# Newton steps ahead of the gate product, landmark products and second query scores at other half steps, a later split

## The chip, the cores and the metric

The kernel runs on one core of a Trainium2 chip. TensorE (PE) does the matrix products into PSUM, VectorE (DVE) and ScalarE (ACT) read and write PSUM and SBUF, GpSimd (POOL) works on SBUF alone, SyncE (SP) issues most DMAs. Every engine works through its own queue in the order in which the program was written; engines wait for each other by semaphores. The metric is the device time of one execution in microseconds, the median of a few runs: 1493.46 us before the change (1492.28 to 1493.96, three runs). TensorE has two clock levels, 1.2 and 2.4 GHz; the profile shows which was granted.

## The reference

A landmark (Nystrom) attention over 8 batches of 8 heads with 576 positions and 32 landmarks, and then two feed-forward layers over the 4608 tokens. Cut to what is computed:

```python
q_lm = q.reshape(B, H, 32, 18, D).mean(axis=3)      # landmarks; k_lm alike
A, Bm, C = sm(q, k_lm), sm(q_lm, k_lm), sm(q_lm, k)  # scaled softmaxes
Z = Bm.T / (norm_1(Bm) * norm_inf(Bm) + 1e-6)
for _ in range(6):
    Z = 2 * Z - Z @ Bm @ Z                           # Newton steps
x = A @ Z @ C @ v                                    # tokens x 512
x = ((x @ w1) * (x @ w2)) @ w3 @ w_out               # gated layer, 1024 wide
h = x @ w_in
out = where(h > 0, h, exp(min(h, 0)) - 1) @ w_out2   # second layer, 2048 wide
```

## The kernel before

All instructions are written in one hand-made order (a manual schedule); no scheduler moves them. The order is what this case is about.

**Folding.** The attention output is never built. For each batch the kernel makes z = Z C v (a 32-landmark matrix per head) and multiplies it by the first-layer weights: the *landmark products* M = z w12, in four column blocks jn = 0 to 3 (`m_tiles`). A batch then has A (the *query scores*, softmaxed and transposed, in two halves of 288 positions) and M, and the two products of the gated layer are A M. w3 and w_out are multiplied into one matrix before.

**Units and half steps.** The first layer runs over 128 units: 8 batches, two halves of positions, eight blocks of 128 columns. In the kernel of before, a unit u does: `ab(u)`, 12 matmuls of the two gate factors into two PSUM tiles (tag `mm`, two buffers), then a copy of the first factor by ScalarE (`a`) and the gate product by VectorE (`g`); `ab_split(u - 1)`, which splits the product before into a high part `gh` (ScalarE) and a low part `gl` (VectorE); then `fill(b, 2 i)`, with i the unit's number in its batch; `yy(u - 2)`, 12 matmuls by the folded w3; `fill(b, 2 i + 1)`. So a batch has 16 units and 32 half steps, hs 0 to 31.

**What fills the half steps.** `fill` emits the attention steps of the next batch that `steps` puts at this half step, those of the own batch that are put at hs + 32, a stage of the conversion of second-layer weights (`conv_job`, worked on by ACT, DVE and POOL and started at hs 1, 5, 11, 14 and 18), and landmark products (`m_at`: half steps 24, 26, 28 and 30 of the batch before; for the first batch's jn 2 and 3 `m_first`). The steps that matter here: `b_norms2` at 11 ends with a first write of X; `r0` at 12 multiplies on TensorE and writes the rest of X on VectorE; `newton` 0 to 5 at 13 to 18, each a TensorE product `n` and a VectorE write of the next X; `zcv` at 21; and for each half of the query scores `a_scores` (TensorE, then two VectorE transposes into `at`), `a_max`, `a_sub`, `a_exp`, `a_sum`, `a_mul` (a product and a transpose into `atf`), `a_split` (ScalarE `ath`, GpSimd `atl`).

**What couples them.** Products of the attention steps share two PSUM buffers (tag `at`): landmark products and query scores take both at a time. A landmark product's buffers are free when VectorE has written its low part (`ml`; it is emitted after `yy`, by `flush`), those of the query scores when VectorE has transposed them. In the last batch the attention's SBUF is given to the second layer: at unit 1 `att_ctx.close()`, from then on five weight loads (`load_w2`, POOL's queue), at unit 2 `load_y(0)` (SP's queue), at units 5 to 8 `split_y(0, ...)`, which splits the loaded y on ScalarE (`yh`) and VectorE (`yl`). After the units, 144 units of the second layer run (`hh`, `oo`).

Of the kernel before, what the change touches and what calls it, by code (L numbers as in the profile page):

```python
# [17 lines left out]
B, H, S, D = 8, 8, 576, 64  # L18
# [6 lines left out]
NP = H // 2  # L25
# [4 lines left out]
KD = DM // 128  # L30
# [9 lines left out]
N1 = 18  # L40
# [10 lines left out]
M2 = 5  # L51
M3 = 10
# [10 lines left out]
def nystrom_moe_kernel(ctx, tc, qT, kT, vm, vr, w12, w3T, w_out1, w_in2, w_out2, out):  # L63
# [3 lines left out]
    def split(hi, lo, src):  # L67
        act.copy(hi, src)  # L68
        dve.tensor_tensor(lo, src, hi.bitcast(F32), op=ALU.subtract)  # L69
# [133 lines left out]
    def load_in(b, which):  # L203
        if which == "v":
            t = att.tile([128, 5, DM], F32, name=f"v{b}", tag="v")
            sp.dma_start(out=t[:, 0:4, :], in_=vm[b])
            sp.dma_start(out=t[0:64, 4, :], in_=vr[b])
        else:
            t = att.tile([128, NP, S], F32, name=f"{which}{b}", tag=which)
            sp.dma_start(out=t, in_=(kT if which == "k" else qT)[b])  # L210
        loaded.setdefault(b, {})[which] = t
# [4 lines left out]
    def flush():  # L216
        while later:
            later.pop(0)()


    class Attention:
# [239 lines left out]
        def steps(self, first=False):  # L461

            s = {}

            def at(i, f, *a):
                s.setdefault(i, []).append((f, a))

            for hp in range(NP):
                at((-16, -14, -12, -11)[hp], self.sums, "k", hp)
                at(hp, self.sums, "q", hp)  # L470
            at(4, self.q_pad)
            at(6, self.b_scores)
            at(7, self.b_exp)
            at(7, self.c_scores, 0)
            at(8, self.c_scores, 1)
            at(8, self.b_soft)
            at(9, self.c_max, 0)
            at(9, self.c_exp, 0)
            at(10, self.b_norms)
            at(10, self.c_max, 1)  # L480
            at(10, self.c_exp, 1)
            at(11, self.b_norms2)
            at(12, self.r0)
            at(13, self.c_norm)
            for k in range(6):
                at(13 + k, self.newton, k)
            for k in range(3):
                at(11 + 2 * k, self.c_trans, k)
            at(18, self.cv, 0)
            at(19, self.cv, 1)  # L490
            at(21, self.zcv)
            when = ((22, 23, 24, 25, 26, 27), (27, 29, 29, 30, 31, 33))
            if first:
                when = ((11, 12, 13, 14, 15, 16), (17, N1, N1 + 1, N1 + 2, N1 + 3, N1 + 4))
            for n, o in enumerate(when):
                at(o[0], self.a_scores, n)
                at(o[0], self.a_max)
                at(o[1], self.a_sub)
                at(o[2], self.a_exp)
                at(o[3], self.a_sum)  # L500
                at(o[4], self.a_mul, n)
                at(o[5], self.a_split, n)
            return s

    atp_ctx = ExitStack()
# [4 lines left out]
    with tc.manual_schedule():  # L510
# [5 lines left out]
        def run_steps(st, i):  # L516
            for f, a in st.get(i, ()):
                f(*a)
# [23 lines left out]
        w12_done = set()  # L542
# [49 lines left out]
        atts = [Attention(b) for b in range(B)]  # L592
        steps = [a.steps(a.b == 0) for a in atts] + [{}, {}]
        a0, st0 = atts[0], steps[0]
# [8 lines left out]
        i = 0  # L603
# [19 lines left out]
        gt = {}  # L623
        accs = {}

        def ab(u):
            b, n, fc = units[u]
            jn, f2 = divmod(fc, 2)
            ah, al = AT[b, n]
            pab = []  # L630
            for w in range(2):
                p = ps_mm.tile([128, 512], F32, name=f"ab{u}_{w}", tag="mm")
                cs = slice(w * 256 + f2 * 128, w * 256 + f2 * 128 + 128)
                for blk in range(2):
                    mh, ml = M_hi[b, jn, blk], M_lo[b, jn, blk]
                    pe.matmul(p[:, :NH], mh[:, cs], ah[:, blk, :], start=(blk == 0), stop=False)  # L636
                    pe.matmul(p[:, :NH], mh[:, cs], al[:, blk, :], start=False, stop=False)  # L637
                    pe.matmul(p[:, :NH], ml[:, cs], ah[:, blk, :], start=False, stop=(blk == 1))  # L638
                pab.append(p)
            a_sb = mlp.tile([128, NH], F32, name=f"a{u}", tag="a_sb", bufs=2)  # L640
            act.copy(a_sb, pab[0][:, :NH])  # L641
            g = mlp.tile([128, NH], F32, name=f"g{u}", tag="g", bufs=2)
            dve.tensor_tensor(g, pab[1][:, :NH], a_sb, op=ALU.mult)  # L643
            hi = mlp.tile([128, NH], F32R, name=f"gh{u}", tag="gh", bufs=3)
            lo = mlp.tile([128, NH], F32R, name=f"gl{u}", tag="gl", bufs=3)
            gt[u] = (hi, lo, g)

        def ab_split(u):
            split(*gt[u])
# [21 lines left out]
        def load_w2(p, f):  # L671
            t = p.tile([128, 4, DM], F32R, name=f"w2_{f}")
            pool.dma_start(out=t, in_=wd[f])
            w2[f] = t
# [20 lines left out]
        def load_y(i):  # L695
            for oc in range(KD):
                y = p2r.tile([128, TB], F32, name=f"yin{i}{oc}", tag="yin", bufs=4)
                sp.dma_start(out=y, in_=yd[:, oc, i * TB : (i + 1) * TB])
                ys[i, oc] = y

        def split_y(i, oc):
            if oc == 0:
                yh[i] = (
                    p2r.tile([128, KD, TB], F32R, name=f"yh{i}", tag="yh", bufs=2),
                    p2r.tile([128, KD, TB], F32R, name=f"yl{i}", tag="yl", bufs=2),
                )
            split(yh[i][0][:, oc, :], yh[i][1][:, oc, :], ys[i, oc])
# [53 lines left out]
        for jn in range(2):  # L761
            a0.m_tiles(jn)
            flush()
        m_at = {24: 0, 26: 1, 28: 2, 30: 3}
        m_first = {M2: 2, M3: 3}

        def fill(b, hs):
            run_steps(steps[b + 1], hs)
            run_steps(steps[b], hs + 32)
            run_steps(steps[b + 2], hs - 32)  # L770
            if pipe.busy():
                pipe.tick()
            else:
                pipe2.tick(hs in CONV)
            if w3o_out:
                split(*w3o_out.pop(0))
            mt = [(atts[b + 1], m_at[hs])] if b + 1 < B and hs in m_at else []
            if b == 0 and hs in m_first:
                while (m_first[hs], NP - 1) not in w12_done:
                    pipe.tick()  # L780
                mt.append((a0, m_first[hs]))
            for a, jn in mt:
                a.m_tiles(jn)

        for u in range(nu + LAG):
            if u < nu:
                b, n, fc = units[u]
                i = n * K1 + fc
                ab(u)
            flush()  # L790
            if 1 <= u <= nu:
                ab_split(u - 1)
            if u < nu:
                fill(b, 2 * i)
                if b + 2 < B and i in (6, 11, 14):
                    load_in(b + 2, {6: "k", 11: "v", 14: "q"}[i])
                if b == B - 1 and i == 1:
                    assert not pipe2.busy()
                    att_ctx.close()
                    p2r = ctx.enter_context(tc.tile_pool(name="p2r", bufs=1, side="right"))  # L800
                if b == B - 1 and 1 <= i <= N_RIGHT:
                    load_w2(p2r, i - 1)
                if b == B - 1 and i == 2:
                    load_y(0)
                if b == B - 1 and 5 <= i < 5 + KD:
                    split_y(0, i - 5)
            else:
                hh(u - nu)
            if u >= LAG:
                yy(u - LAG)  # L810
            flush()
            if u < nu:
                fill(b, 2 * i + 1)
# [8 lines left out]
        for u in range(LAG, n2 + LAG2):  # L822
            if u < n2:
                i, f = units2[u]
# [59 lines left out]
```

## Time and profile before

| what | value |
|---|---|
| median of three runs | 1493.46 us (1492.28 to 1493.96) |
| the profiled execution | 1495.25 us, of it a span of 1493.5 us from first to last instruction |
| TensorE busy | 1421.6 us, 95% of the span |
| VectorE, ScalarE, GpSimd busy | 879.8, 699.5, 251.1 us |
| mean granted clock of TensorE | 0.984 of the full 2.4 GHz |
| stretch 0 to 131 us (start, weights folded) | TensorE busy 90.87 us |
| stretch 131 to 187 us (first batch) | 45.44 of 56 us |
| stretch 187 to 640 us (steady batches) | 440.25 of 453 us |
| stretch 640 to 699 us (last batch, change to the second layer) | 55.66 of 59 us |
| stretch 699 us to the end (second layer) | 789.33 of 794.5 us |

A steady batch lasts about 70 us. The page's chain of work gives TensorE 79% of the span and VectorE 15%. A matmul's end is modelled, so its duration overlaps with the next one; what counts on TensorE is the distance from start to start.

### The profile page before, as it was taken

To read this page: it belongs to the slowest core of one execution; us is meant where nothing else is said; L and a number is where in the kernel's file an instruction comes from. 1 tells how busy PE (TensorE), PEld (TensorE's weight loads), DVE (VectorE), ACT (ScalarE), POOL (GpSimd) and SP (SyncE) were. 2 spreads that over 40 slices of the span, in tenths; PEclk is the share of its full clock that TensorE was granted. 3 is DMA by queue.
4 is the path that set the end of the run, shared out by engine and by line. 5 is a ranking of instruction groups with operands and counts; after the bars stand their busy time and mean duration, and the time that the engine had idled before them with its cause. 6 is when DMAs were issued, how large, how long until landed. Compare 5 with 4: busy or idle time off the path is not lost.

```text
span 1493.5 us, 23710 instructions
## 1 busy us (share of the span) xinstructions
PE 1421.6 (95%) x9552; PEld 1144.8 (77%) x9552; DVE 879.8 (59%) x1719; ACT 699.5 (47%) x1333; POOL 251.1 (17%) x231
## 2 busy tenths in 40 slices
PE   4786899999999999999999999999999999999998
PEld 1234788788787878898888888888888888888886
DVE  8888686777767676633544545454454545445443
ACT  5664344544444444334444445454444545444443
POOL 4554234242323233201000000000000000000000
PEclk9888999999999999999999999999999999999999
DMA  7553244444343432152601010100101001010000
GB/s 288 181 183 117 91 137 152 136 161 151 133 162 135 153 137 88 45 201 101 253 0 57 1 57 1 42 15 1 57 1 57 1 11 47 1 57 0 29 0 29
DMA packets 40302, 129.46 MB, mean 87 GB/s; under 512 B 3840, under 2 KB 12032, under 8 KB 35072
## 3 DMA queue, kind: packets, MB, share of 16 engines
q1 hardware_dynamic: 37888, 111.16, 21.4%
q0 software_dynamic: 2304, 16.78, 2.9%
q8 instruction: 75, 1.23, 0.3%
q14 instruction: 35, 0.29, 0.1%
HBM read 92.27 MB, written 35.65 MB: 86 GB/s over the span
## 4 chain that ended last, share of the span: by engine, by line
PE 79%; DVE 15%; ACT 2%; issue 2%; DMA 2%; SPq 0%; DVEq 0%; ACTq 0%
PE o L747 9%; PE o L749 9%; PE o L748 9%; PE h L719 9%; PE h L718 9%; PE h L720 9%; PE ab L636 4%; PE y L659 3%; PE ab L637 3%; PE ab L638 3%; PE y L661 3%; PE y L660 3%; PE w3acc L524 2%; DVE gl L69 2%; DVE w_p L146 2%
## 5 line engine op out<-in xcount | busy, mean ns | idle before, releaser
L747 PE MATMUL o<-w,eh 128*128 128x512 f32 x576 | 226.9, 394 | 0.7 <-ACT ysb L665 0.7
L719 PE MATMUL h<-yl,w 128*128 128x512 f32 x576 | 227.0, 394 | 0.0
L749 PE MATMUL o<-w,el 128*128 128x512 f32 x576 | 226.9, 394 | 0.0
L748 PE MATMUL o<-w,eh 128*128 128x512 f32 x576 | 226.7, 394 | 0.0
L718 PE MATMUL h<-yh,w 128*128 128x512 f32 x576 | 226.4, 393 | 0.0
L720 PE MATMUL h<-yh,w 128*128 128x512 f32 x576 | 226.3, 393 | 0.0
L728 DVE SCALAR_TENSOR_TENSOR t<-m,t 128x512 f32<-128x512 f32 x144 | 99.8, 693 | 196.2 <-ACT m L727 196.2
L68 ACT CAST eh<-t 128x512 fp32r<-128x512 f32 x144 | 89.4, 621 | 213.8 <-DVE t L729 213.8
L636 PE MATMUL ab<-ath,mh 128*128 128x288 f32 x512 | 158.4, 309 | 3.8 <-ACT a L641 2.7
L659 PE MATMUL y<-gh,w3oh 128*128 128x288 f32 x512 | 159.9, 312 | 1.5 <-DVE w3ol L69 1.5
L69 DVE TENSOR_TENSOR el<-t,eh 128x512 fp32r<-128x512 f32 x144 | 99.8, 693 | 98.8 <-ACT eh L68 98.8
L637 PE MATMUL ab<-atl,mh 128*128 128x288 f32 x512 | 152.7, 298 | 0.0
L638 PE MATMUL ab<-ath,ml 128*128 128x288 f32 x512 | 152.0, 297 | 0.0
L661 PE MATMUL y<-gh,w3ol 128*128 128x288 f32 x512 | 151.2, 295 | 0.0
L660 PE MATMUL y<-gl,w3oh 128*128 128x288 f32 x512 | 150.9, 295 | 0.1
L724 ACT COPY hs<-h 128x512 f32<-128x512 f32 x144 | 84.5, 587 | 99.7 <-PE h L720 99.6
L643 DVE TENSOR_TENSOR g<-ab,a 128x288 f32<-128x288 f32 x128 | 57.8, 452 | 120.0 <-ACT gh L68 62.5
L747 PEld LDWEIGHTS o<-w,eh 128*128 128x128 f32 x576 | 108.2, 188 | 26.3 <-ACT ysb L665 1.1
L719 PEld LDWEIGHTS h<-yl,w 128*128 128x128 f32 x576 | 108.0, 188 | 25.6
L718 PEld LDWEIGHTS h<-yh,w 128*128 128x128 f32 x576 | 108.0, 188 | 25.4
L749 PEld LDWEIGHTS o<-w,el 128*128 128x128 f32 x576 | 108.1, 188 | 25.2
L720 PEld LDWEIGHTS h<-yh,w 128*128 128x128 f32 x576 | 108.1, 188 | 25.1
(132 smaller groups left out, 2460.4 us busy)
## 6 DMA issues: line engine op xcount, KB each, us to landing
wd<-w2c SPq DMA_DIRECT2D x32, 512.0 KB, 3.5
w<-wd POOLq DMA_DIRECT2D x16, 1024.0 KB, 14.4
k<-in_kT_dram SPq DMA_DIRECT2D x8, 1152.0 KB, 7.4
q<-in_qT_dram SPq DMA_DIRECT2D x8, 1152.0 KB, 5.2
yd<-ysb SPq DMA_DIRECT2D x16, 576.0 KB, 3.7
yin<-yd SPq DMA_DIRECT2D x36, 256.0 KB, 3.9
out_dram<-osb SPq DMA_DIRECT2D x36, 256.0 KB, 2.2
w_raw<-in_w3T_dram SPq DMA_DIRECT2D x16, 512.0 KB, 5.2
```

What stands on the lines that cost most here:

```text
L636: pe.matmul(p[:, :NH], mh[:, cs], ah[:, blk, :], start=(blk == 0), stop=False)
L637: pe.matmul(p[:, :NH], mh[:, cs], al[:, blk, :], start=False, stop=False)
L638: pe.matmul(p[:, :NH], ml[:, cs], ah[:, blk, :], start=False, stop=(blk == 1))
L659: pe.matmul(a[oc][:, :NH], w3o_hi[fc][:, os_], gh, start=(fc == 0), stop=False)
L660: pe.matmul(a[oc][:, :NH], w3o_hi[fc][:, os_], gl, start=False, stop=False)
L661: pe.matmul(a[oc][:, :NH], w3o_lo[fc][:, os_], gh, start=False, stop=(fc == K1 - 1))
L718: pe.matmul(p[:, :TB], w2[f][:, 0, kk * 128 : (kk + 1) * 128], yhi[:, kk, :], start=(kk == 0), stop=False)
L719: pe.matmul(p[:, :TB], w2[f][:, 0, kk * 128 : (kk + 1) * 128], ylo[:, kk, :], start=False, stop=False)
L720: pe.matmul(p[:, :TB], w2[f][:, 1, kk * 128 : (kk + 1) * 128], yhi[:, kk, :], start=False, stop=(kk == KD - 1))
L747: pe.matmul(a, eh[:, ts_], w2[f][:, 2, :], start=(f == 0), stop=False)
L748: pe.matmul(a, eh[:, ts_], w2[f][:, 3, :], start=False, stop=False)
L749: pe.matmul(a, el[:, ts_], w2[f][:, 2, :], start=False, stop=(f == K2 - 1))
```

## The change

Four edits. First, `ab` is cut in two: `ab(u)` emits the 12 matmuls, `ab_product(u)` the copy and the gate product, and between them `quick` emits those steps of this even half step that are `r0` or `newton` (they are then taken off the list). Second, of the four landmark products jn 0 is at 24 as before, jn 1 at 28, and jn 2 and 3 are at half steps 0 and 2 of the batch that they belong to. Third, the scores of the second half of the queries are at 26, their later steps at 27, 28, 29, 30, 32 and 34 (before: scores and maximum 27, then 29, 29, 30, 31, 33); the first half keeps its places. Fourth, `split_y` of the last batch is at units 9 to 12.

```diff
-            when = ((22, 23, 24, 25, 26, 27), (27, 29, 29, 30, 31, 33))
+            when = ((22, 22, 23, 24, 25, 26, 27), (26, 27, 28, 29, 30, 32, 34))
...
                 pab.append(p)
+            gt[u] = pab
+
+        def ab_product(u):
+            pab = gt[u]
...
-        m_at = {24: 0, 26: 1, 28: 2, 30: 3}
-        m_first = {M2: 2, M3: 3}
+        m_own, m_next, m_first = {0: 2, 2: 3}, {24: 0, 28: 1}, {M2: 2, M3: 3}
+
+        def quick(b, hs):
+            st = steps[b + 1].get(hs, [])
+            for s in [s for s in st if s[0].__name__ in ("r0", "newton")]:
+                st.remove(s)
+                s[0](*s[1])
...
-            mt = [(atts[b + 1], m_at[hs])] if b + 1 < B and hs in m_at else []
-            if b == 0 and hs in m_first:
-                while (m_first[hs], NP - 1) not in w12_done:
+            mt = [(atts[b + 1], m_next[hs])] if b + 1 < B and hs in m_next else []
+            own = m_own if b else m_first
+            if hs in own:
+                while (own[hs], NP - 1) not in w12_done:
                     pipe.tick()
-                mt.append((a0, m_first[hs]))
+                mt.append((atts[b], own[hs]))
...
                 ab(u)
+                quick(b, 2 * i)
+                ab_product(u)
...
-                if b == B - 1 and 5 <= i < 5 + KD:
-                    split_y(0, i - 5)
+                if b == B - 1 and 9 <= i < 9 + KD:
+                    split_y(0, i - 9)
```

VectorE's queue around half steps 11 to 13 of the second batch, first before, then after (X is the Newton iterate, r and n the PSUM products of `r0` and `newton`):

```order
L338 TENSOR_TENSOR X_2468<-bm_2314,brc_2464 128x2x32
L643 TENSOR_TENSOR g_2495<-ab_1_2486,a_2493 128x288
L69 TENSOR_TENSOR gl_2435<-g_2432,gh_2434 128x288
L347 TENSOR_TENSOR X_2468<-r_2_2501,brc_2464 128x2x32
L284 TENSOR_SCALAR csum_2405<-csum_2405 128x2
L286 RECIPROCAL crs_2526<-csum_2405 128x2
L359 SCALAR_TENSOR_TENSOR X_2529<-X_2468,n_2_2528 128x128
```

```order
L338 TENSOR_TENSOR X_2468<-bm_2314,brc_2464 128x2x32
L347 TENSOR_TENSOR X_2468<-r_2_2493,brc_2464 128x2x32
L647 TENSOR_TENSOR g_2505<-ab_1_2486,a_2503 128x288
L69 TENSOR_TENSOR gl_2435<-g_2432,gh_2434 128x288
L284 TENSOR_SCALAR csum_2405<-csum_2405 128x2
L286 RECIPROCAL crs_2526<-csum_2405 128x2
L359 SCALAR_TENSOR_TENSOR X_2529<-X_2468,n_2_2528 128x128
```

The write of X from r0 now stands ahead of the gate product and the low part; the same holds for newton 1, 3 and 5, and the other Newton writes stay where they were.

VectorE's queue from half step 26 on, before (a_2 and m_2 are the PSUM tiles of scores and landmark products):

```order
L449 TENSOR_TENSOR at_2881<-at_2881,asum_2972 128x576
L451 STREAM_TRANSPOSE atf_2999<-at_2881 128x576
L418 TENSOR_TENSOR ml_1_0_3013<-m_2_3002,mh_1_0_3012 128x512
L418 TENSOR_TENSOR ml_1_1_3016<-m_2_3003,mh_1_1_3015 128x512
L427 STREAM_TRANSPOSE at_3036<-a_2_3037 128x288
L427 STREAM_TRANSPOSE at_3036<-a_2_3038 128x288
L432 TENSOR_REDUCE amx_3049<-at_3036 128x18
L643 TENSOR_TENSOR g_3067<-ab_1_3058,a_3065 128x288
L69 TENSOR_TENSOR gl_2995<-g_2992,gh_2994 128x288
L418 TENSOR_TENSOR ml_2_0_3084<-m_2_3073,mh_2_0_3083 128x512
L418 TENSOR_TENSOR ml_2_1_3087<-m_2_3074,mh_2_1_3086 128x512
L435 TENSOR_TENSOR at_3036<-at_3036,amx_3049 128x576
```

The same place after the change:

```order
L449 TENSOR_TENSOR at_2881<-at_2881,asum_2972 128x576
L451 STREAM_TRANSPOSE atf_2999<-at_2881 128x576
L427 STREAM_TRANSPOSE at_3001<-a_2_3002 128x288
L427 STREAM_TRANSPOSE at_3001<-a_2_3003 128x288
L432 TENSOR_REDUCE amx_3031<-at_3001 128x18
L647 TENSOR_TENSOR g_3049<-ab_1_3040,a_3047 128x288
L69 TENSOR_TENSOR gl_2995<-g_2992,gh_2994 128x288
L435 TENSOR_TENSOR at_3001<-at_3001,amx_3031 128x576
L418 TENSOR_TENSOR ml_1_0_3067<-m_2_3056,mh_1_0_3066 128x512
L418 TENSOR_TENSOR ml_1_1_3070<-m_2_3057,mh_1_1_3069 128x512
```

The low parts of jn 1 no longer stand between the first half's last transpose and the second half's scores.

VectorE's queue at the turn to the next batch (half steps 0 to 2) after the change; before, it held there only g, gl and the four sums of q (qsum):

```order
L647 TENSOR_TENSOR g_3143<-ab_1_3134,a_3141 128x288
L69 TENSOR_TENSOR gl_3108<-g_3105,gh_3107 128x288
L241 TENSOR_REDUCE qsum_3149<-q_3072 128x32
L449 TENSOR_TENSOR at_3001<-at_3001,asum_3111 128x576
L451 STREAM_TRANSPOSE atf_3152<-at_3001 128x576
L418 TENSOR_TENSOR ml_2_0_3165<-m_2_3154,mh_2_0_3164 128x512
L418 TENSOR_TENSOR ml_2_1_3168<-m_2_3155,mh_2_1_3167 128x512
L241 TENSOR_REDUCE qsum_3149<-q_3072 128x32
L647 TENSOR_TENSOR g_3203<-ab_1_3194,a_3201 128x288
L69 TENSOR_TENSOR gl_3146<-g_3143,gh_3145 128x288
L241 TENSOR_REDUCE qsum_3149<-q_3072 128x32
L418 TENSOR_TENSOR ml_3_0_3225<-m_2_3214,mh_3_0_3224 128x512
```

The product and transpose of the second half and the low parts of jn 2 and 3 moved here. The orders of POOL and SP are the same in both kernels, but for the line numbers.

## Rows read from the trace of the kernel before

**Rows 1.** Busy time by stretch: us, then each engine's busy us (instructions), clock, DMA
```profile
187.00:640.00 453.00, 440.25 (x4766) 375.08 (x4765) 326.16 (x759) 206.65 (x486) 157.56 (x141) 1.00 0.38 134
```

**Rows 2.** Who waited for whom, whole span: us in total, times, longest
```profile
PEld a L256 <- DVE ml L418: 9.6, 14, 1.3
...
PE n L357 <- DVE csum L284: 7.7, 6, 1.3
...
PE ab L636 <- ACT a L641: 2.7, 1, 2.7
...
PEld m L256 <- DVE at L427: 2.0, 8, 0.6
```

**Rows 3.** Timeline of TensorE, newton 0: start us, us, instruction, [idle before]
```profile
236.84 0.43 PE L357 MATMUL n<-X 32*32 32x64 f32 x16 [1.29 <-DVE csum L284]
```

**Rows 4.** Timeline of VectorE at the same place
```profile
234.79 0.23 DVE L338 TENSOR_TENSOR X<-bm,brc 128x64 f32<-128x64 f32 x1
235.73 0.46 DVE L643 TENSOR_TENSOR g<-ab,a 128x288 f32<-128x288 f32 x1 [0.71 <-ACT a L641]
236.11 0.45 DVE L69 TENSOR_TENSOR gl<-g,gh 128x288 fp32r<-128x288 f32 x1
236.47 0.22 DVE L347 TENSOR_TENSOR X<-r,brc 128x64 f32<-128x64 f32 x1
```

**Rows 5.** Timeline of ScalarE at the same place
```profile
234.83 0.57 ACT L373 COPY ct<-ct 128x512 f32<-128x512 f32 x1
```

**Rows 6.** Timeline of TensorE, half steps 22 to 30 (first matmul of each block)
```profile
257.54 0.72 PE L256 MATMUL a<-q,ksum 64*32 64x288 f32 x16
...
264.68 0.29 PE L636 MATMUL ab<-ath,mh 128*128 128x288 f32 x1
...
266.37 1.09 PE L256 MATMUL m<-w_sb,z 64*32 64x512 f32 x16
267.39 0.40 PE L659 MATMUL y<-gh,w3oh 128*128 128x288 f32 x1
...
270.13 1.31 PE L256 MATMUL a<-q,ksum 64*32 64x288 f32 x16 [0.89 <-DVE ml L418]
...
275.87 0.30 PE L636 MATMUL ab<-ath,mh 128*128 128x288 f32 x1
```

**Rows 7.** Timeline of VectorE, half steps 24 to 33
```profile
264.90 1.28 DVE L418 TENSOR_TENSOR ml<-m,mh 128x512 fp32r<-128x512 f32 x2
...
267.94 0.75 DVE L449 TENSOR_TENSOR at<-at,asum 128x576 f32<-128x576 f32 x1
268.72 0.78 DVE L451 STREAM_TRANSPOSE atf<-at 128x576 f32<-128x576 f32 x1
...
271.52 0.85 DVE L427 STREAM_TRANSPOSE at<-a 128x288 f32<-128x288 f32 x2 [0.84 <-PE a L256]
...
277.95 0.46 DVE L643 TENSOR_TENSOR g<-ab,a 128x288 f32<-128x288 f32 x1 [1.04 <-ACT a L641]
...
283.27 1.40 DVE L241 TENSOR_REDUCE qsum<-q 128x32 f32<-128x576 f32 x2
```

**Rows 8.** Timeline of TensorE, two units that nothing holds
```profile
280.27 0.29 PE L636 MATMUL ab<-ath,mh 128*128 128x288 f32 x1
...
283.47 0.30 PE L636 MATMUL ab<-ath,mh 128*128 128x288 f32 x1
```

**Rows 9.** Timeline of GpSimd
```profile
248.66 1.16 POOL L155 TENSOR_TENSOR w_t<-w_t,w_s 128x512 f32<-128x512 f32 x1 [1.75 <-DVE w_s L148]
...
283.43 1.44 POOL L458 TENSOR_TENSOR atl<-atf,ath 128x576 fp32r<-128x576 f32 x1 [11.74 <-ACT ath L457]
```

**Rows 10.** Timeline of VectorE beside the first row of GpSimd
```profile
248.80 1.33 DVE L69 TENSOR_TENSOR gl<-g,gh 128x288 fp32r<-128x288 f32 x1
```

**Rows 11.** Timeline of ScalarE in the last batch, first split of y
```profile
654.25 0.62 ACT L68 CAST yh<-yin 128x512 fp32r<-128x512 f32 x1 [6.47 <-DMA yin<-yd]
```

**Rows 12.** Timeline of TensorE at the same place
```profile
655.22 0.40 PE L636 MATMUL ab<-ath,mh 128*128 128x288 f32 x1 [2.69 <-ACT a L641]
```

More of the change, by code (lines that the diff above doesn't have):

```diff
@@ L491, in steps @@
             at(21, self.zcv)
-            when = ((22, 23, 24, 25, 26, 27), (27, 29, 29, 30, 31, 33))
+            when = ((22, 22, 23, 24, 25, 26, 27), (26, 27, 28, 29, 30, 32, 34))
             if first:
-                when = ((11, 12, 13, 14, 15, 16), (17, N1, N1 + 1, N1 + 2, N1 + 3, N1 + 4))
+                when = ((11, 11, 12, 13, 14, 15, 16), (17, 17, N1, N1 + 1, N1 + 2, N1 + 3, N1 + 4))
             for n, o in enumerate(when):
                 at(o[0], self.a_scores, n)
[L497 to L502, printed above, removed]
+                at(o[1], self.a_max)
+                at(o[2], self.a_sub)
+                at(o[3], self.a_exp)
+                at(o[4], self.a_sum)
+                at(o[5], self.a_mul, n)
+                at(o[6], self.a_split, n)
             return s
```

## The prediction

> **What bounds the kernel now.** I read the stretches first. From 187 to 640 us, six and a half batches of the first layer, TensorE is busy 440.25 of 453 us at a granted clock of 1.00, the 2.4 GHz level; VectorE has 326 us of work there, ScalarE 207, GpSimd 158 [rows 1]. So TensorE's own products set the time, the change takes none of them away, and all that can be won there by order is what TensorE waits: 12.75 us of idle time, and a little more that hides in overlapping durations. Second I read who waited for whom, for the places of this idle time [rows 2]. Three places carry it. The loads of the query scores' weights wait 9.6 us in 14 waits for landmark low parts (the second half's scores of seven batches, two PSUM buffers each). Newton 0 waits 7.7 us in six batches for VectorE. And once, in the last batch, a gate product waits 2.7 us for ScalarE. The second layer, more than half of the span, is not touched. Third I read the timelines around one case of each place, in the batch that runs from 210 to 280 us.
>
> **Newton first (quick).** The Newton product of half step 13 starts at 236.84 after 1.29 us of idle time, which so began at 235.55 [rows 3]. What it waits for is the second write of X, which ended at 236.69, 0.15 us before it [rows 4]. That write stood behind a gate product, which itself waited for ScalarE's copy until 235.73, and a low part. But the first write of X was over at 235.02, and r0's product was long done. Moved up, the second write follows there: 235.02 + 0.22 + 0.15 = 235.39, before TensorE gets there at all. The next thing that could hold Newton 0 is its PSUM buffer, which ScalarE's copy of the transposes frees at 234.83 + 0.57 = 235.40 [rows 5], with the same 0.15 us 235.55: just in time. So the wait goes, all 7.7 us of it, and at most 0.1 us in each of six batches comes back (0 to 0.6; I take 0). The other side of the move: at half steps 12, 14, 16 and 18 the gate product now stands behind a Newton write of 0.2 to 0.3 us that waits for its product on TensorE. The gate product is needed only by the second half of the next unit's matmuls, more than a unit's half away, and newton 1, 3 and 5 held nobody before. I cost this at nothing; the cover is the 12 matmuls of y, about 1.6 us.
>
> **Second scores at half step 26.** Before, they stood at 27, right behind the jn 1 product of 26, whose low parts VectorE got to only after the first half's transposes; they started at 270.13 and got their second buffer later still [rows 6]. Now they take the place in which the jn 1 product ran at 266.37 without a wait, with the same need: two buffers, freed by the jn 0 low parts at 264.90 + 1.28 = 266.18 [rows 7]. So they run at 266.37 too, with 0.2 us to spare, and the 9.6 us go. What is late next is the jn 1 product at 28, which needs the buffers of these scores. VectorE: first half's last transpose to 268.72 + 0.78 = 269.50, then two transposes of the scores, 0.85 [rows 7], free at 270.35, seen 0.1 later. TensorE: 266.37 + 0.72 for the scores + 1.69 for y + 1.69 for the gate matmuls (12 matmuls beside other work, 264.68 to 266.37) = 270.47 [rows 6]. Again just in time; 0 to 0.2 us in each of seven batches, I take 0.
>
> **Landmark products 2 and 3 at the turn.** TensorE's part is moved, not added. VectorE's part moves from the tail of a batch to the first two units of the next: a product and a transpose (0.75 + 0.78) and four low parts (2 x 1.28), 4.1 us [rows 7], beside the four sums of q. I count from the start of the batch's first gate matmuls. TensorE: 1.69, jn 2 1.02 (266.37 to 267.39), y 1.69, gate 1.69, so it comes to jn 3 at 6.09. VectorE: the gate product starts 2.08 after its matmuls began (275.87 to 277.95 [rows 6, 7]), then by start-to-start distances 0.38 and 0.36 [rows 4], a sum of q 0.70, the product 0.78, the transpose 0.78, two low parts 1.28 [rows 7]: 6.36. The first of jn 3's two buffers is free at 5.7, the second some 0.3 us after TensorE wants it. I take 0.2 us, in seven batches 1.4; bounds 0 and 0.4, so 0 to 2.8. The next link holds: VectorE does the second unit's gate product at about 7.5, and the third unit's matmuls need it at 6.3 + 1.02 + 1.69 + 0.8 = 9.8.
>
> On that slack a rule speaks against the change. GpSimd's low part of the second scores (1.44 us [rows 9]) moves into the second unit too, half step 34. The trace shows what such a neighbour does: a low part on VectorE takes 0.45 us alone [rows 4] and 1.33 us while GpSimd works on a weight tile [rows 9, 10]. The Trainium skill, SBUF — State Buffer, section Who interferes with whom, says that a VectorE instruction with two SBUF inputs and a GpSimd instruction that reads SBUF exclude each other for a whole instruction; by that rule, with which these rows agree, the first unit's low part waits up to 1.44 us there. By it alone the sum stays as it is, because 9.8 - 7.5 = 2.3 us are free; without the slack it would be the second rival's.
>
> **The later split.** ScalarE waited 6.47 us, until 654.25, for the loaded y [rows 11], with the copy for the gate product behind it, and TensorE lost 2.69 us [rows 12]. It came to the split at 647.8. Four units later are 4 x 3.20 us (280.27 to 283.47 [rows 8]), plus two landmark products of 1.02 that are new in this batch: 662.6 against a landing at 654.25. The release of the attention's memory is later as well, since jn 3 and the last GpSimd part now end in unit 1 rather than 0: at most a unit and two products, 5.2 us, so the landing is at 659.5 at the latest. The wait of 2.7 us goes. The split halves are needed at the end of the units, more than three units on.
>
> **The sum.** 7.7 + 9.6 + 2.7 = 20.0 less 1.4 is 18.6 us. The profiled execution has a span of 1493.5 of its 1495.25 us, and nothing outside the span changes; the span agrees with the median, so I subtract from the median: 1493.46 - 18.6 = 1474.9. The differences that a measurement of this kernel can tell are about 0.2%, 3 us.
>
> **Rivals.**
> 1. *A new wait takes the place of part of the old one.* Two links above are just in time and one is late. If one of them is late by a collision with GpSimd of the size shown, 1.33 - 0.45 = 0.88 us, in each of seven batches, 6.2 us come back: 1481. For it: VectorE runs without a pause there. Against: the jn 1 product ran unheld in the same place.
> 2. *Newton doesn't move what it should.* If Newton 0 is held by the copy of the transposes or another wait as long as before, only 9.6 + 2.7 - 1.4 = 10.9 us go: 1482.6. Against: the copy ended 1.4 us before Newton 0 started.
> 3. *More goes.* The first landmark product waits 2.0 us in all for the scores' transposes [rows 2]. If the new phase frees that too and jn 3 is not held: 1493.46 - 22 = 1471.5.
> 4. *Slower.* VectorE doesn't drain at the turn, and all of the 4.1 us moved there lies on TensorE's path in seven batches: 28.7 - 20.0 = 8.7 us more, 1502. It decides from the point at which the second unit's gate product is later than 9.8 us, 2.3 us later than worked out. Against: VectorE pauses before the gate product in plain units (1.04 us in one case, [rows 7]), and before the change its sums of q ran with no other attention work beside them.
>
> **How the numbers follow.** Forecast 0.60 (1473 to 1477), rival 1 0.18, rival 2 0.06, rival 3 0.06, rival 4 0.05; 0.05 for a mixture around 1487 to 1492. The range leaves out the last two and the far half of rival 2: 1471 to 1482. Faster by over 0.2% are the forecast, the first three rivals and a little of the mixture: 0.91; within 0.2% 0.04; slower 0.05.
>
> **What would show it.** In the profile after: who waited for whom has no row of Newton 0 for VectorE over 1 us in total and none of the scores' weight loads over 2 us; in its place a row of landmark products waiting for low parts or transposes of 1 to 2 us; the split in the last batch without a wait for the load; TensorE idle about 2 us rather than 12.75 in the steady batches, and a batch 2.6 us shorter. Wrong would be: landmark waits of 6 us or more (rival 1), Newton 0 still idle before its start (rival 2), gate matmuls in units 1 to 3 waiting for the gate product (rival 4), or a second layer that is no longer 794 us.

## The result, and the profile after

The changed kernel takes 1474.38 us (median of four runs, 1473.62 to 1475.18) against 1493.41 us before in the same session: a ratio of 0.9874 with an interval of 0.9856 to 0.9891, or 19.0 us less. The forecast was 1474.9 us. The profiled execution has a span of 1472.3 of its 1474.1 us and a mean granted clock of 0.984, as before.

The stretch of the steady batches comes first again. It is shorter by a bit more than two microseconds and a half per batch, so the cut is at 621 instead of 640 us (start and end, length, then busy us and instructions of TensorE, its weight loads, VectorE, ScalarE, GpSimd; clock, DMA share, GB/s):

```profile
187.00:621.00 434.00, 433.82 (x4751) 372.60 (x4750) 332.31 (x757) 202.96 (x485) 158.09 (x141) 1.00 0.39 137
```

Before, TensorE was busy 440.25 of 453 us there, with almost the same count of instructions [rows 1]. Its 12.75 us of idle time are down to 0.18 us; VectorE has as many instructions and 6 us more of busy time, the others about the same. Who waited for whom in the kernel after (us in total, times, longest):

```profile
PEld m L256 <- DVE at L427: 2.2, 10, 0.4
...
PE n L357 <- DVE X L359: 0.8, 2, 0.5
...
PEld a L256 <- DVE ml L418: 0.7, 4, 0.2
...
PE m L256 <- DVE at L427: 0.2, 1, 0.2
```

The scores' weight loads wait 0.7 us where they waited 9.6; Newton 0 has no row of its own any more (the 0.8 us belong to two Newton products ahead of the first gate matmuls, at 86.75 and 95.22 us, which wait for the write of another Newton step); the gate product's wait of 2.7 us is gone; and the 2.0 us of the landmark weight loads stayed, 2.2 [rows 2].

The timeline of TensorE in the same batch (start us, us, instruction; the first matmul of each block):

```profile
233.47 0.42 PE L357 MATMUL n<-X 32*32 32x64 f32 x16
...
258.31 1.45 PE L256 MATMUL m<-w_sb,z 64*32 64x512 f32 x16
...
263.09 0.71 PE L256 MATMUL a<-q,ksum 64*32 64x288 f32 x16
...
267.11 1.18 PE L256 MATMUL m<-w_sb,z 64*32 64x512 f32 x16
268.22 0.40 PE L663 MATMUL y<-gh,w3oh 128*128 128x288 f32 x1
...
273.10 0.29 PE L636 MATMUL ab<-ath,mh 128*128 128x288 f32 x1
...
279.18 1.14 PE L256 MATMUL m<-w_sb,z 64*32 64x512 f32 x16
280.25 0.40 PE L663 MATMUL y<-gh,w3oh 128*128 128x288 f32 x1
```

No line carries a bracket with an idle time. Newton 0 (233.47) had 1.29 us of it before [rows 3], the second scores (263.09) 0.89 [rows 6]. Small holds remain in the durations: the landmark product at 267.11 is followed by y after 1.11 us and that at 279.18 after 1.07, where a free one takes 1.02. VectorE at these places:

```profile
232.78 0.22 DVE L338 TENSOR_TENSOR X<-bm,brc 128x64 f32<-128x64 f32 x1
232.92 0.22 DVE L347 TENSOR_TENSOR X<-r,brc 128x64 f32<-128x64 f32 x1
233.71 0.46 DVE L647 TENSOR_TENSOR g<-ab,a 128x288 f32<-128x288 f32 x1 [0.58 <-ACT a L645]
...
266.30 0.85 DVE L427 STREAM_TRANSPOSE at<-a 128x288 f32<-128x288 f32 x2
...
274.96 0.46 DVE L647 TENSOR_TENSOR g<-ab,a 128x288 f32<-128x288 f32 x1 [1.20 <-ACT gh L68]
...
277.92 1.25 DVE L418 TENSOR_TENSOR ml<-m,mh 128x512 fp32r<-128x512 f32 x2
...
280.11 1.55 DVE L69 TENSOR_TENSOR gl<-g,gh 128x288 fp32r<-128x288 f32 x1
```

Both writes of X now stand side by side (232.78, 232.92), and only then does VectorE wait for ScalarE's copy (0.58 us). Before, it waited 0.71 us with the second write still behind the gate product [rows 4]. The turn to the next batch is the lower half: gate product 274.96, low parts from 277.92 to 279.17. ScalarE, the copy of the transposes and the first split of y:

```profile
232.82 0.57 ACT L373 COPY ct<-ct 128x512 f32<-128x512 f32 x1
...
642.27 0.62 ACT L68 CAST yh<-yin 128x512 fp32r<-128x512 f32 x1
```

GpSimd, the last low part of A and the first of the five weight loads that follow the attention:

```profile
279.92 1.43 POOL L458 TENSOR_TENSOR atl<-atf,ath 128x576 fp32r<-128x576 f32 x1 [11.53 <-ACT ath L457]
...
618.11 2.83 POOL L677 DMA_DIRECT2D w<-wd  x5 [0.31 <-PE y L665]
```

The split of y no longer waits for its load (6.47 us before [rows 11]).

To put the gain into places without depending on idle brackets, I took the distance from the first matmul of each block on TensorE to that of the next, from the first gate matmuls to the second layer, and summed it by kind of block (both kernels have the same number of each):

| blocks, start to start | after less before |
|---|---|
| y ahead of a Newton product (45.82 to 37.75 us, 21 blocks) | -8.1 us |
| y ahead of the late gate product in the last batch | -2.7 |
| other y (-5.9 ahead of the second scores, which start on time; +0.8 in the rest) | -5.1 |
| scores | -4.2 |
| gate matmuls | -0.6 |
| landmark products | +0.6 |

Unrounded, that is 19.97 us less. From the first gate matmuls to the last instruction it is 1368.60 us before and 1348.63 after, 19.97 less as well: the places account for all of it. The 0.8 us in the rest of the y come in the main from one more y per batch that has landmark products or scores next to it: such a y takes 1.69 us to the next start, one between two blocks of gate matmuls 1.60. The time ahead of the first gate matmuls was 124.85 and 123.70 us in these two executions, with no edit in it, and lies between 121.5 and 124.9 in the executions of this study. So the experiments are compared by this distance, called *the distance* below, and by their medians. A second execution of the kernel after has a distance of 1349.09 us, so half a microsecond in it tells nothing.

### The profile page after: what moved, and what is told of

It reads as the page before. It is cut to its first block, busy times and chain, and to the rows that moved or that the text cites. A ratio compares the mean times of both kernels' runs of the same rounds, so it can differ in the third digit from the quotient of the medians.

```text
span 1472.3 us, 23676 instructions
## 1 busy us (share of the span) xinstructions
PE 1417.4 (96%) x9552; PEld 1144.7 (78%) x9552; DVE 887.3 (60%) x1719; ACT 696.1 (47%) x1333; POOL 252.4 (17%) x231
## 4 chain that ended last, share of the span: by engine, by line
PE 90%; DVE 7%; issue 1%; ACT 1%; DMA 1%; SPq 0%; DVEq 0%; ACTq 0%
PE o L751 9%; PE o L753 9%; PE o L752 9%; PE h L723 9%; PE h L722 9%; PE h L724 9%; PE y L663 5%; PE ab L636 5%; PE ab L637 4%; PE ab L638 4%; PE y L665 4%; PE y L664 4%; PE m L256 2%; PE w3acc L524 2%; PE n L357 1%
## 5 line engine op out<-in xcount | busy, mean ns | idle before, releaser
L751 PEld LDWEIGHTS o<-w,eh 128*128 128x128 f32 x576 | 108.2, 188 | 26.2 <-ACT ysb L669 1.1
L752 PEld LDWEIGHTS o<-w,eh 128*128 128x128 f32 x576 | 108.2, 188 | 24.7
```

The costliest lines, as they stand in the source:

```text
L751: pe.matmul(a, eh[:, ts_], w2[f][:, 2, :], start=(f == 0), stop=False)
L752: pe.matmul(a, eh[:, ts_], w2[f][:, 3, :], start=False, stop=False)
```

## The experiments

All start from the kernel after; diffs are against it. The first three each undo one part.

**The Newton writes back behind the gate product.**

```diff
-                quick(b, 2 * i)
```

> The changed kernel with the Newton steps and r0 back behind the gate product in VectorE's queue; the other edits stay. Theory (the write of X behind the gate product is the whole cause of Newton 0's wait, and nothing else takes its place when it is there): Newton 0 idle about 1.3 us in six batches again, 7.7 us by the row of waits, 8.1 us by start-to-start distances, so 1474.4 + 8 = 1482.4 us (1481.5 to 1483.5). Rival (with landmark products elsewhere VectorE reaches that place earlier, or the time lost is caught up behind it): less than half of it, 1474.5 to 1478.

Measured: 1480.94 us (1480.34 to 1483.15), 0.9917 of before (0.9902 to 0.9932); the distance is 1356.81, 8.2 us more than after. Waits and timeline of this kernel:

```profile
PE n L357 <- DVE csum L284: 7.6, 6, 1.3
```

```profile
233.98 0.42 PE L357 MATMUL n<-X 32*32 32x64 f32 x16 [1.29 <-DVE csum L284]
```

The median lies just under the expected 1481.5 to 1483.5. The row of before came back with its count and its length, 1.29 us at one start (before: 7.7, 6, 1.3 [rows 2, 3]). The step is right and worth what was said.

**The split of y back at units 5 to 8.**

```diff
-                if b == B - 1 and 9 <= i < 9 + KD:
-                    split_y(0, i - 9)
+                if b == B - 1 and 5 <= i < 5 + KD:
+                    split_y(0, i - 5)
```

> The changed kernel with the split of y in the last batch back at units 5 to 8. Theory A (the loads now start later, since the attention's memory is released one unit later): the weight loads are issued 8.7 us after the last batch's first gate matmuls instead of 4.9, so ScalarE meets the split at about 629.2 and y lands at about 637.4, a wait of 8 us instead of 6.5 and 4.3 us on TensorE: 1478.7 us. Theory B (the edit is worth what the wait of before was): 2.7 us, 1477.1 us.

Measured: 1479.8 us (1478.34 to 1480.67), 0.9906 (0.9891 to 0.9921); the distance 1354.74, 6.1 us more than after and not the 2.7 us that the split cost before. ScalarE and TensorE at the place, then the stretches around it:

```profile
636.92 0.62 ACT L68 CAST yh<-yin 128x512 fp32r<-128x512 f32 x1 [8.01 <-DMA yin<-yd]
```

```profile
637.89 0.40 PE L636 MATMUL ab<-ath,mh 128*128 128x288 f32 x1 [4.23 <-ACT a L645]
```

```profile
633.00:638.00 5.00, 0.77 (x7) 0.55 (x6) 0.43 (x1) 1.08 (x3) 0.00 (x0) 1.00 0.77 295
638.00:640.00 2.00, 2.00 (x10) 2.00 (x11) 1.60 (x4) 1.23 (x4) 0.00 (x0) 0.58 0.01 5
640.00:642.00 2.00, 2.00 (x11) 2.00 (x10) 1.09 (x3) 0.71 (x2) 0.00 (x0) 0.57 0.00 0
642.00:644.00 2.00, 2.00 (x17) 2.00 (x16) 0.33 (x1) 0.24 (x1) 0.00 (x0) 1.00 0.00 0
```

Two things make the 6.1. The first is that the loads start later: the first weight load is issued 8.7 us after the last batch's first gate matmuls (618.11 against 609.42 in the kernel after, and as much here) where it was 4.9 before, so ScalarE waits 8.01 instead of 6.47 us and TensorE 4.23 instead of 2.69. Both tables of the change delay it. With the scores at their old place alone (run further down) the load is at 7.8 us, with the landmark products at theirs alone at 7.5, with both at 4.9; in the kernel after it stands in GpSimd's queue right behind the last low part of A, whose place moved with the scores. The second is the clock. After that idle time TensorE ran at the 1.2 GHz level from 638.3 to 641.7 us (the granted clock is 0.58 and 0.57 over the two middle stretches, which hold a bit of full clock each), in which only 10 or 11 matmuls fit into 2 us instead of 17: that is the rest, 1.9 us. By kind of block the 6.1 us are 4.9 in y (4.23 idle), 1.0 in gate matmuls and 0.2 in landmark products. In the kernel before, the same place shows no such fall:

```profile
652.00:655.00 3.00, 0.54 (x5) 0.31 (x3) 0.10 (x1) 0.75 (x2) 0.00 (x0) 1.00 0.78 298
655.00:657.00 2.00, 1.78 (x13) 1.78 (x14) 1.93 (x4) 1.66 (x5) 0.00 (x0) 1.00 0.02 9
```

So this edit is the one whose worth depends on another: with the landmark products and scores in their new places it is worth 5.4 us by the medians and 6.1 by the distance; with the old places it would have been worth the 2.7 us of the wait before, which no run tried by itself.

**Landmark products and scores at their old places.**

```diff
-            when = (..., (26, 27, 28, 29, 30, 32, 34))
+            when = (..., (27, 27, 29, 29, 30, 31, 33))
...
-        m_own, m_next, m_first = {0: 2, 2: 3}, {24: 0, 28: 1}, {M2: 2, M3: 3}
+        m_own, m_next, m_first = {}, {24: 0, 26: 1, 28: 2, 30: 3}, {M2: 2, M3: 3}
```

> The changed kernel with landmark products at 24, 26, 28, 30 of the batch before and second scores at 27, as before; Newton steps ahead and the later split stay. Theory (the scores' wait for buffers is worth 9.6 to 10 us, and the new places cost under 1 us of their own): 1474.4 + 9.3 = 1483.7 us (1482.5 to 1485). Rival (part of the wait only existed because Newton 0 had delayed TensorE against VectorE, or the new places cost 2 us or more): 1480 us or less, or 1486 and more.

Measured: 1483.46 us (1482.81 to 1484.09), 0.9931 (0.9916 to 0.9946); the distance 1357.27, 8.6 us more. Waits of this kernel:

```profile
PEld a L256 <- DVE ml L418: 9.4, 14, 1.1
```

The 14 waits are back with their size [rows 2]. By kind of block: 5.0 us more in y, 4.2 in the scores, 0.2 in gate matmuls, and 0.6 less in landmark products. The 5.0 are 5.7 more in the y ahead of the second scores and 0.7 less in others, so the new places cost about 1.3 us by themselves, a little more than the 1 us that was expected at most.

**Only the write of r0 ahead.** Is it the second write of X alone, or the writes of Newton 1, 3 and 5 as well?

```diff
-            for s in [s for s in st if s[0].__name__ in ("r0", "newton")]:
+            for s in [s for s in st if s[0].__name__ == "r0"]:
```

> The changed kernel with only r0's write of X ahead of the gate product; Newton 1, 3 and 5 back behind it. Theory (only the write of half step 12 was waited for): no difference, 1474.4 us within 1 us, and no idle time before any Newton product. Rival (the odd Newton steps were close to the path and their new place is part of the gain): 1476 us or more, with idle time before Newton 2 or 4.

Measured: 1472.8 us (1472.6 to 1474.62), 0.9864 (0.9847 to 0.988), the distance 1349.33, 0.7 us more than after; no idle time ahead of Newton 0. The median is 1.6 us lower than after's, a bit more than the 1 us that was expected, and the distance goes the other way. The gain is r0's write; the three others can't be told from no change.

**Second scores back at 27, landmark products as after.** The two tables of the change were moved together. This run and the next take them apart.

```diff
-            when = (..., (26, 27, 28, 29, 30, 32, 34))
+            when = (..., (27, 27, 29, 29, 30, 31, 33))
```

> The changed kernel with the second half's scores back at 27 (their later steps at 27, 29, 29, 30, 31, 33 as before); landmark products stay at 24, 28, 0 and 2. Theory (the wait came from the jn 1 product standing between the jn 0 product and the scores; once that is at 28, the scores' place at 26 or 27 doesn't matter, since TensorE comes to the jn 1 product at the same time either way and VectorE's queue holds the same work ahead of it): 1474.4 us within 1 us, no wait of the scores, and the 0.05 us wait of jn 3 at the turn gone because the product and transpose are ahead of the turn again. Rival (the place 26 is itself part of the gain): 1477 us or more, with waits of the scores or of jn 1.

Measured: 1473.75 us (1473.07 to 1475.0), 0.9862 (0.9847 to 0.9876), the distance 1348.70 against 1348.63. No row of the scores' weight loads waiting for low parts is left. The hold of jn 3 at the turn is gone too, as expected. So the half step of the scores is worth nothing by itself: the 9 us come with the landmark products' new places. The row that is gone names the low parts that the scores waited for, those of jn 1 at 26; jn 1 was not moved without jn 2 and 3.

**Second scores at 26, landmark products at their old places.** The other half alone: the scores take the two PSUM buffers first, and the jn 1 product of the same half step follows directly.

```diff
-        m_own, m_next, m_first = {0: 2, 2: 3}, {24: 0, 28: 1}, {M2: 2, M3: 3}
+        m_own, m_next, m_first = {}, {24: 0, 26: 1, 28: 2, 30: 3}, {M2: 2, M3: 3}
```

> The changed kernel with the landmark products back at 24, 26, 28, 30 of the batch before, and the second scores at 26 all the same. Theory (two pairs of PSUM buffers in one half step, one of them behind VectorE's transposes): the jn 1 product follows the scores directly and wants their buffers at once, but VectorE has transposed them only 3.4 us later; seven batches, 24 us, less 0.8 us of small waits that go: 1497.5 us (1494 to 1500), slower than the kernel before. Rival (moving the scores forward is what helps): 1480 us or less.

Measured: 1507.59 us (1505.96 to 1508.18), 1.0085 of before (1.007 to 1.010), the distance 1381.92, 33.3 us more than after. It missed its number, 1497.5, and even its bound of 1500. Waits, timeline and one stretch of this kernel:

```profile
PE m L256 <- DVE at L427: 20.8, 8, 3.1
```

```profile
268.89 0.71 PE L256 MATMUL a<-q,ksum 64*32 64x288 f32 x16
...
272.68 1.45 PE L256 MATMUL m<-w_sb,z 64*32 64x512 f32 x16 [3.08 <-DVE at L427]
```

```profile
274.20:276.80 2.60, 2.60 (x11) 2.60 (x12) 1.95 (x3) 1.65 (x3) 0.86 (x1) 0.50 0.48 191
```

The wait itself came nearly as expected, six times 2.9 to 3.1 us and 2.41 in the last batch. What was left out is the clock: behind each of the seven the granted clock goes to 0.50, the 1.2 GHz level, for about 3.4 us (6.8 in the first batch). The last of them and a stretch behind it:

```profile
631.77 2.13 PE L256 MATMUL m<-w_sb,z 64*32 64x512 f32 x16 [2.41 <-DVE at L427]
```

```profile
632.50:635.50 3.00, 3.00 (x22) 1.67 (x8) 0.95 (x2) 1.57 (x3) 0.00 (x0) 0.50 0.00 0
```

By kind of block against the kernel after, the scores (up to the held landmark product) take 21.0 us more, y 6.8, landmark products 5.2, gate matmuls 0.2: 33.2 together. The first is the wait; the 12 us behind it, a third of the loss, fall into the blocks at the lower clock, though part of the landmark products' 5.2 can also be their second buffer.

**Landmark jn 3 half a unit earlier at the turn.** The prediction had the third link of its chain, VectorE at the turn, at 0.2 us behind TensorE. How much slack is in it?

```diff
-        m_own, m_next, m_first = {0: 2, 2: 3}, {24: 0, 28: 1}, {M2: 2, M3: 3}
+        m_own, m_next, m_first = {0: 2, 1: 3}, {24: 0, 28: 1}, {M2: 2, M3: 3}
```

> The changed kernel with the jn 3 product at half step 1 instead of 2 of its batch. Theory (at the turn VectorE's queue, not TensorE, sets when the two buffers are free): TensorE comes to jn 3 at 4.4 us after the batch's first gate matmuls instead of 6.1, the second buffer is free at 6.1 as before, so 1.7 us of waiting in seven batches, 12 us: 1486.4 us (1484 to 1488). Rival (VectorE has the slack to free them earlier): under 1478 us.

Measured: 1483.4 us (1482.41 to 1484.0), 0.9927 (0.991 to 0.9943), the distance 1358.80, 10.2 us more than after. The median lies just under the expected 1484 to 1488.

```profile
PE m L256 <- DVE ml L418: 8.2, 8, 2.1
```

```profile
278.44 1.69 PE L256 MATMUL m<-w_sb,z 64*32 64x512 f32 x16 [0.97 <-DVE ml L418]
```

```profile
277.73 1.25 DVE L418 TENSOR_TENSOR ml<-m,mh 128x512 fp32r<-128x512 f32 x2
```

One of the 8 waits, 2.1 us long, is ahead of the first gate matmuls and in the kernel after too. The others are as that of 278.44: the product starts when the first buffer is free, after 0.97 us, and then waits within its 1.69 us for the second (low parts end at 277.73 + 1.25 = 278.98). By kind of block the 10.2 us are 6.6 in y, ahead of the product, and 3.7 in landmark products, less 0.1 in gate matmuls. In the kernel after, y and the next gate matmuls, 1.69 us each, stand between jn 2 and jn 3; here only y does, and that is too little cover for VectorE's work at the turn.

**Transposes of the first scores ahead of the low part of the gate product.** In the kernel after, the landmark product of 24 still lasts longer than 1.02 us in four batches (258.31: 1.38 until the next start), because VectorE reaches the transposes late, behind a low part that runs beside GpSimd. Here the scores of half step 22 are written ahead of the gate product's split:

```diff
+        def early(b):
+            st = steps[b + 1].get(22, [])
+            if st:
+                f, a = st.pop(0)
+                f(*a)
...
                 ab_product(u)
+                if i == 11:
+                    early(b)
```

> The changed kernel with the first half's scores (half step 22) emitted between the gate product and the low part of the unit, so that their transposes stand ahead of the low part in VectorE's queue. Theory (the first landmark product's wait of 0.3 to 0.4 us in four or five batches, 1.7 us in all, comes from that low part, which GpSimd holds up to 1.35 us): the wait goes, 1472.7 us (1471.5 to 1473.5), and by start-to-start distances the landmark product at 24 takes 1.02 us in every batch. Rival (the low part, now later, holds the next unit): 1474.4 us or more.

Measured: 1471.41 us (1470.59 to 1472.58), 0.9846 (0.9831 to 0.986), the distance 1346.47, 2.2 us less than after, and the median a touch under the expected 1471.5 to 1473.5. TensorE and VectorE of this kernel, then VectorE of the kernel after:

```profile
258.21 1.09 PE L256 MATMUL m<-w_sb,z 64*32 64x512 f32 x16
```

```profile
256.57 0.84 DVE L427 STREAM_TRANSPOSE at<-a 128x288 f32<-128x288 f32 x2
...
257.33 0.58 DVE L69 TENSOR_TENSOR gl<-g,gh 128x288 fp32r<-128x288 f32 x1
```

```profile
256.52 1.34 DVE L69 TENSOR_TENSOR gl<-g,gh 128x288 fp32r<-128x288 f32 x1
...
257.78 0.83 DVE L427 STREAM_TRANSPOSE at<-a 128x288 f32<-128x288 f32 x2
```

The transposes are done at 257.41 instead of 258.61, and the product takes 1.02 us to the next start in every batch. The kernels after and this one ran once more on one chip, with the next kernel:

> The changed kernel itself, on the same chip as the two that follow, so that they can be compared with it: 1474.4 us within 1.5 us (theory and rival alike).

> The first half's scores between gate product and low part, once more, beside the changed kernel: 2 us less than it by the distances from the first gate matmuls to the end (1346.5 against 1348.6 us); by the times 1 to 3 us less. Rival (the 3 us between the earlier medians were the chip or the start): no difference.

Measured: after 1473.35 us (1471.79 to 1474.95), 0.9862 (0.9847 to 0.9877); this kernel 1472.19 (1471.96 to 1473.08), 0.9856 (0.984 to 0.9873). The ranges overlap, so by times alone the step can't be told from no change; the distance is 2.6 us shorter again (1346.52 against 1349.09).

**The first batch's jn 3 ahead of the transposes.** The largest wait left behind the first gate matmuls is in the first batch: TensorE's transposes of e wait 4.5 us for the low parts of the landmark product jn 3. That product runs early enough (152.92 us), but its copy on ScalarE stands behind an exponential that itself waits for VectorE. Here the product, its copies and low parts are written ahead of the other steps of that half step.

```diff
         def fill(b, hs):
+            if b == 0 and hs == M3:
+                while (m_first[hs], NP - 1) not in w12_done:
+                    pipe.tick()
+                a0.m_tiles(m_first[hs])
+                flush()
             run_steps(steps[b + 1], hs)
...
-            if hs in own:
+            if hs in own and (b or hs != M3):
```

It holds the step of the kernel before it as well.

> The kernel of the run before with one more move in the first batch alone: the jn 3 product of half step 10, its copies and low parts stand ahead of the other steps of that half step. Theory (the 4.5 us of the first transposes' wait come from the high part's copy, which ScalarE does only behind an exponential that itself waits for VectorE's maximum): the low parts end 2 to 3 us earlier, and the first batch is 2.6 us shorter: 79.2 us instead of 81.8 from first gate matmuls to first gate matmuls, 1469 us or 2 to 3 us less than the run before. Rival (the maximum and the norms, now behind the low parts, hold r0 or the exponential instead): no gain.

Measured: 1466.78 us (1464.96 to 1467.66), 0.9817 (0.9802 to 0.9831), the distance 1341.26, 7.8 us less than after on the same chip and 5.3 less than the kernel with the early transposes alone. The kernel after, ScalarE, TensorE and the stretches of the first batch:

```profile
158.17 0.78 ACT L277 ACTIVATE e<-e,cb 128x576 f32<-128x576 f32 x1 [2.46 <-DVE cb L274]
...
158.95 1.05 ACT L417 CAST mh<-m 128x512 fp32r<-128x512 f32 x2
```

```profile
160.29 1.12 PE L368 MATMUL ct<-ident,e 128*128 128x128 f32 x4 [4.50 <-DVE ml L418]
```

```profile
154.00:158.00 4.00, 1.79 (x14) 1.55 (x12) 2.62 (x10) 1.48 (x4) 0.00 (x0) 0.98 0.70 278
158.00:164.50 6.50, 4.21 (x32) 3.94 (x32) 2.28 (x8) 3.14 (x7) 0.00 (x0) 0.50 0.00 0
```

The kernel of this experiment:

```profile
153.86 1.07 ACT L417 CAST mh<-m 128x512 fp32r<-128x512 f32 x2
```

```profile
155.22 0.66 PE L368 MATMUL ct<-ident,e 128*128 128x128 f32 x4 [1.22 <-DVE ml L418]
```

```profile
155.20:162.00 6.80, 6.78 (x78) 6.14 (x78) 4.60 (x19) 3.46 (x9) 0.00 (x0) 1.00 0.01 2
```

The wait falls from 4.50 to 1.22 us, and the clock behind it stays at 1.00, where the kernel after shows 0.50, the 1.2 GHz level, for 6.5 us, 2.3 of them still idle. The first batch takes 76.56 instead of 81.8 us: 5.2, twice the 2.6 that were expected. Of these 3.3 are the shorter wait itself. The other 2.0 lie almost all in the blocks behind it, 1.3 of them in gate matmuls, which ran at half clock in the kernel after and run at full clock here. This is the fastest kernel of the study, 0.9817 of before.

## Why the prediction was right, point by point

**The bound** was read rightly: of the 12.75 us that TensorE stood idle in the steady batches 0.18 are left (the prediction said about 2), and a steady batch is 2.2 to 3.0 us shorter (the second 67.52 instead of 70.23; 2.6 was said).

**Newton first: 7.7 us said, 8.1 measured** (8.2 by undoing it). The buffer was just in time, as worked out: ScalarE's copy ends at 232.82 + 0.57 = 233.39, and Newton 0 starts at 233.47, at its turn, with no bracket. That the gate product behind it costs nothing held too.

**Second scores: 9.6 said, 9.3 measured** (5.1 + 4.2; by undoing it 9.2, 5.0 + 4.2). The held places alone gave 5.9 + 4.2 = 10.1, and 0.8 came back in other y, which the prediction had not looked for. And the step's name for its cause did not hold. The prediction gave the gain to the scores' new half step; with the landmark products alone in their new places the time is the same (1473.75), and with the scores alone in theirs it is 1507.59. The gain goes with the landmark products' places: jn 1, whose low parts the scores waited for, left half step 26. Its own working did name the right link, the two buffers. The jn 1 product at 28, said to be held 0 to 0.2 us, is held 0.09 in the batch shown (267.11 to 268.22 is 1.11; the transposes end at 266.30 + 0.85 = 267.15) and up to 0.13 in others.

**The turn: -1.4 us said, -0.3 measured.** This is the term that was most mis-sized. The jn 3 product was to be held 0.2 us in each of seven batches; it is held about 0.05 in six (279.18 to 280.25 is 1.07; the low parts end at 277.92 + 1.25 = 279.17). The walk had the batch's gate product 2.08 us after its matmuls; in the turn shown it starts 1.86 after them (273.10 to 274.96), which is 0.22 of the 0.29 us by which the second buffer is early against the walk (6.07 instead of 6.36). All that landmark products lose after the change, at any half step, is 0.6 us more than before; the other 0.3 are the holds of jn 1 at 28, taken as 0.

**The weighed rule.** The batch's second low part takes 1.55 us at 280.11, beside GpSimd's 1.43 us at 279.92, against 0.45 alone [rows 4]. That is the longer of the two outcomes that were weighed, and it costs TensorE nothing, as worked out: the gate matmuls two blocks on are at their usual distance. The Trainium skill, SBUF — State Buffer, section Who interferes with whom, has such a pair exclude each other; here the two began 0.19 us apart and VectorE's ended 0.31 us after GpSimd's, with which the rule agrees. (For the case without slack the prediction named its second rival; the collision is weighed in its first.)

**The later split: 2.7 us said and measured.** The load was in time: the split starts at 642.27 without a wait. That a later release of memory would matter was seen, but only as a bound on the landing; the experiment shows that without the later split this would have cost 6.1 us.

**The sum** was 20.0 less 1.4, 18.6 us. By places it is 8.1 + 9.3 + 2.7 + 0.6 (gate matmuls) - 0.6, unrounded 20.0; by the medians 19.0. The executions' differing starts, up to 3.3 us with no edit in them, are more than what lies between these numbers. So that forecast and median agree within 0.6 us is in part luck: by places the sum was 1.4 us short.

**The rivals.** No new wait took the old one's place (0.6 us and not 6.2). More did not go: the first landmark product's 2.0 us of waits stayed as 2.2, and the kernel with early transposes shows what they needed, a place of the transposes ahead of the low part. The slower case did not come: its point was a gate product of the second unit later than 9.8 us after the batch's first gate matmuls, and it starts at 6.65 (279.75). VectorE's work at the turn can get on TensorE's path, but by the buffers: with jn 3 half a unit earlier it did, for 10.2 us.

## What to carry to other kernels

Where engines share few PSUM buffers through in-order queues, write down for each product who frees its buffers and when, and place the products so that enough other matmuls lie between any two that hand the same buffers on. Here two blocks of 1.69 us (y and gate matmuls) covered almost all of VectorE's work. With y alone between them, jn 1 and the second scores lost 9 us before the change, and jn 2 and jn 3 lost 10 in an experiment; with nothing between, scores and jn 1 lost 33, clock included. One block was enough only where VectorE had little to do: the gate matmuls between scores at 27 and jn 1 at 28. Move an instruction that another engine waits for ahead of one that itself waits (the second write of X ahead of the gate product). Price a wait of TensorE of some microseconds with the clock behind it: one that was cut from 4.50 to 1.22 us, 3.3 less, gave back 5.2.

## What the runs showed of the hardware

The granted clock went to 0.50 behind idle times of TensorE of 2.41 to 3.08 us (seven, scores at 26 with the old landmark places), 4.23 us (split at 5 to 8) and 4.50 us (first batch of the kernel after), and stayed full behind 2.69 us (before), 1.29 and 1.22 us. Since it fell behind 2.41 us and not behind 2.69, the length of the idle time alone does not decide it. The stretch at the lower level was about 3.4 us after the 4.23 us and after six of the seven, and 6.8 us after the first of the seven; in the first batch of the kernel after 0.50 stands over 6.5 us, in 2.3 of which TensorE was still idle. On what this hangs was not tried.
